# A planner's keys set anew in a fused banded-attention and feed-forward kernel

## The chip, the cores and the metric

The kernel runs on one core of one Trainium2 chip. The metric is device time in microseconds (us): the median of three executions. A separate execution was profiled, and all rows below come from it.

## The reference

The inputs are q, k and v of shape (8 batches, 8 heads, 576 positions, head size 64), and two weight matrices of 512x2048 and 2048x512, all float32. Attention sees a causal band of 64 positions; its output, 4608 tokens of 512 numbers, goes through a feed-forward layer with a piecewise gate.

```python
scores = scale * np.matmul(q, k.transpose(0, 1, 3, 2))
mask = (rel >= 0) & (rel < 64)
scores = np.where(mask, scores, -1000000000.0)
attn = np.exp(scores - np.max(scores, axis=-1, keepdims=True))
attn = attn / (np.sum(attn, axis=-1, keepdims=True) + 1e-09)
x = np.matmul(attn, v)            # to (4608, 512), heads side by side
h = x @ w_in
g = np.where(h >= 1, h, np.where(h <= -1, 0.0, (h + 1) ** 2 / 4))
out = g @ w_out
```

## The kernel before

**Work.** The tokens are 9 tiles of 512 (t = 0 to 8). Attention goes in 36 steps of 128 tokens (s = 0 to 35), four to a tile. The feed-forward layer has 16 slices of 128 hidden numbers (f = 0 to 15). Each float32 matrix is split into a high and a low part, and a product is three matmuls: high by high, high by low, low by high.

**Tiles 0 to 2** run plainly: for each f, `ffn_in` (12 matmuls, L1153, into the two buffers ps_h), then on ScalarE and VectorE relu, square, *gate* (L1175, VectorE; it reads ps_h and so gives it back), `ffn_high` (L1180, gh), `ffn_low` (L1185, gl), then `ffn_out` (12 matmuls, L1199). While tile 0 runs, the raw weights of each f are loaded and split on ScalarE and VectorE (`w_rest` L342, `w_sign` L319, two limits L323, shift L335, join L346, `w_high` L290, `w_low` L358). While tiles 1 and 2 run, 32 *half-sums* of weights (`add_sums`: `sum_whole` L842, `sum_sums` L849, `sum_high` L290 into o, `sum_low` L857, on VectorE or GpSimd) are made and stored to DRAM (`kept`): 16 *passes* `sum_pass` (L824, three transfers each) and two stores for each half-sum (L861, L862).

**Tiles 3 to 8** run in three blocks of two tiles with a scheme of seven products in place of eight (`ffn_product` L928, `out_product` L1014). Their right operands come from `kept` through a ring of seven slots (`ring_load`, L908). What they multiply is made out of four pairs of attention steps (r = 0 to 3) by `add_build` (`x_take`, `x_sums` L587, `x_high`, `x_low` L623); the first product of a block waits for all four.

**Attention steps** from s = 5 on: loads of q, k (L407, L411) and two of v (L417); scores on TensorE (L439); per head half a mask and minimum on VectorE (L462), exp on ScalarE (L482); inverse (L493, L494), normalise (L501), transposition (L508) on VectorE; a write to DRAM and a read back (L519, L522); then the values on TensorE (L552). In tile 2 and the blocks the values of one step stand on TensorE right behind the scores of a later one.

**Order.** Each engine and the queue of SyncE (SP) works in program order, and that order comes from a planner (`Plan.run`) that walks a model with fixed costs before anything is emitted. Each piece of work has a *key*. For each engine the planner takes, among pieces that could start at most PATIENCE after the earliest, the one with the lowest key:

```python
until = min(could)[0] + PATIENCE[e]
c = min((c for c in could if c[0] <= until), key=lambda c: c[1:])
```

Key 0 is the start of tile 0; `step(t)` is 21.33, 42.67 and 64 for t = 1, 2 and 3, that is 1.333 for each f, and block u begins at `64 + 2 * u * H_STEP`. The keys of attention steps are counted backwards from the tile that needs them: in tile 2 the last step (s = 11) has `step(2) - A_END - B_STEP - EARLY_2` and each one before it B_FIRST less; for the first block the last step has `64 - A_SUPER[0][0]`, each one before it `A_SUPER[0][1]` less. Loads of q and k have the step's key less L_LEAD, those of v V_LATE or V_LATE_2 more than that. Half-sum c of pass n (0 to 15) has `step(1) + S_LATE + S_PACE * (n + c / 2)`, the pass that of c = 0. A raw weight load has `W0_KEY + W0_STEP * (f + unit / 2)`.

The first k and the first raw weights are issued on ScalarE's queue ahead of all else; in the planner they are SP work that does nothing (`load_k(s) if s else None`, `FIRST_LOAD`).

Of the kernel before, what the change touches and what calls it, by code (L numbers as in the profile page):

```python
# [40 lines left out]
JOIN = 8  # L41
BEHIND = 2
E_SPAN = 0.29
E_LEAD = 9.81
W_LEAD = -1.5
W_FIRST = (17.22, -2.0, 1.41, 1.48, -3.05)
W_STEP = 1.02
L_LEAD = -0.77
W_LATE = (3.72, -1.06, -2.67, 7.19, 13.28, 13.03, 18.55)
W_LOAD = 1400  # L50
Q_LOAD = 700
K_LOAD = 1040
V_LATE = 2.92
W0_KEY = -100.2
FIRST_LOAD = 0, (0,)
M_LATE = 1
W0_STEP = 12.29
FINE = 4
NWARM = 8
A_FIRST = (-102.6, -95.58, -95.43, -95)  # L60
A_NEXT = 1.57
A_STEP = 4.75
A_SPAN = 2.18
A_LEAD = 4.64
O_LAG = 2.79
O_LAG_DMA = 2300
# [11 lines left out]
B_PE = 2210  # L78
B_DUE = (2.44, -1.28, -0.74)
B_STEP = 5.68  # L80
B_FIRST = 1.45
A_END = 5.86
V_PE = 1270
NORM = dict(Pool=800, DVE=480), dict(DVE=610)
G_LATE = (1.94, 1.65, -4.21, -4.45, 2.08)
D_LATE = (-0.7, 0.46, 6.3, -3.34, 6.37, 0.12)
# [11 lines left out]
SUM_KEEP = 1150  # L98
V_LATE_2 = 14.69
PATIENCE = dict(ACT=300, DVE=0, Pool=303, PE=0, SP=0)  # L100
# [5 lines left out]
SUPERS = 3  # L106
H_STEP = 18.67
S_LATE = 1.62
S_PACE = 2.47
O_CHANGE = 3.33, 3.2, 4.7  # L110
EARLY_2 = 2.71
A_SUPER = ((7.71, 2.68), (9.52, 4.03))
A_ORDER = (0, 4, 1, 5, 2, 6, 3, 7)
BUILD = (-12.04, 16.74)
X_SLOTS = 4, 0, 6, 1, 2, 3
# [3 lines left out]
WRITES = (1, None), (2, 1), (0, None), (3, 2), (3, 3), (1, 2), (2, 2)  # L119
R_LEAD = -4.99  # L120
R_LOAD = 430
L_DVE = 4, 6, 8
G_LEAD = (3.99, -2.67, 0.94, -2.12)
OP_LEAD = 10.45
D_LEAD = 0.72


class Plan:
# [10 lines left out]
    def add(self, key, cost, do, after=(), takes=(), gives=(), lag=0, shared=False):  # L139
        self.work.append((key, cost, do, set(after), takes, gives, lag, shared))  # L140
        return len(self.work) - 1
# [77 lines left out]
def banded_attention_then_ffn(ctx: ExitStack, tc: tile.TileContext, q, k, v, w, masks, out, out_t, dims):  # L219
# [142 lines left out]
    def add_weights(f, units):  # L362
        g = f, units
        m = len(units) * DM
        act, high, join, low, small = 105 + .916 * m, 92 + .844 * m, 10 + 1.22 * m, 67 + 1.05 * m, 90 + .25 * m
        key = f * W_STEP - (W_FIRST[f] if f < len(W_FIRST) else W_LEAD) + .5 * units[0]
        x = add(W0_KEY + W0_STEP * (f + .5 * units[0]), dict(SP=W_LOAD * len(units)), lambda e: None if g == FIRST_LOAD else w_load(g), lag=DMA_LAG)
        xr = add(key - W_LATE[0], dict(ACT=act), lambda e: w_rest(g), [x], takes=["u"])
        x = add(key, dict(ACT=act), lambda e: w_sign(g), [xr])
        x = add(key - W_LATE[1], dict(DVE=small), lambda e: w_limit_signed(g), [x])  # L370
        x = add(key - W_LATE[2], dict(DVE=small), lambda e: w_limit_unsigned(g), [x])
        x = add(key - W_LATE[3], dict(DVE=small), lambda e: w_shift(g), [x])
        x = add(key - W_LATE[4], dict(DVE=join), lambda e: w_join(g), [x])
        x = add(key - W_LATE[5], dict(ACT=high), lambda e: w_high(g, e), [x])
        x = add(key - W_LATE[6], dict(DVE=low), lambda e: w_low(g), [x], gives=[("u", xr)])
        for u in units:
            w_ready[f, u] = x
# [290 lines left out]
    def add_step(t, i):  # L668
# [7 lines left out]
        if s < FIRST:  # L676
            key = due = A_FIRST[s]
        elif s >= JOIN:
            key = a_keys[s]
        else:  # L680
            key = a_keys[s]
            due = min(key + A_SPAN, soon(s))
        lk = key - L_LEAD
        apart = A_SUPER[t > PLAIN][1]
        if s == 0:
            last["r"] = add(lk, dict(ACT=480), lambda e: round_masks())
        if s == PE_STEPS - 2:
            last["m"] = add(lk + M_LATE, dict(SP=590), lambda e: load_masks(), lag=DMA_LAG)
        late = s >= JOIN
        xq = add(lk, dict(SP=Q_LOAD), lambda e: load_q(s), takes=["qt"], lag=Q_LAG if late else DMA_LAG)  # L690
        xk = add(lk, dict(SP=Q_LOAD if late else K_LOAD), lambda e: load_k(s) if s else None, takes=["kt"], lag=K_LAG if late else DMA_LAG)
        vk, vl = lk + (V_LATE_2 if late else V_LATE), V_LAG if late else DMA_LAG
# [58 lines left out]
        else:  # L751
            dk = key if s >= JOIN else min(key + E_SPAN, soon(s) - E_LEAD)
            due = [dk + B_DUE[0], dk + B_DUE[0] + B_DUE[2]]
            x = [add(due[h], dict(DVE=LOWEST), lambda e, h=h: att_masked(s, h), [xs, last["m"]], gives=[(ps, xs, h)]) for h in range(2)]
            x = [add(due[h], dict(ACT=EXP[1]), lambda e, h=h: att_exp(s, h, False), [x[h]]) for h in range(2)]
            x = add(due[1], dict(DVE=430), lambda e: att_inverse(s, BOTH), x)
            x = [add(due[1], dict(DVE=870, Pool=1650) if s >= JOIN else dict(DVE=870), lambda e: att_normalize(s, BOTH, e), [x], shared=True)]
            due = dk + B_DUE[1]
            if s == SOON:
# [444 lines left out]
    def out_late(t, q, i):  # L1204
        if t < PLAIN - 1 or q < NF - 2:
            return O_LAG
        return O_CHANGE[0] if q == NF - 2 else O_CHANGE[1 + i // 2]
# [27 lines left out]
    def soon(s):  # L1235

        t, i = s * SB // TMAX, s * SB % TMAX // SB
        return step(t) + (FRONT * TMAX / 2 / 384 if 2 * i >= TMAX // SB else 0) - A_NEXT + i % 2

# [187 lines left out]
```

## Time and profile before

| | |
|---|---|
| median of three executions | 840.55 us (840.16 to 840.74) |
| the profiled execution's own time | 843.4 us |
| its span, first to last instruction | 841.6 us |
| TensorE busy | 821.6 us, 98% |
| VectorE busy | 687.0 us, 82% |
| ScalarE busy | 533.5 us, 63% |
| GpSimd busy | 213.8 us, 25% |
| moved by DMA | 216.08 MB, mean 257 GB/s |

In the rows PE is TensorE, PEld its weight loads, DVE VectorE, ACT ScalarE, POOL GpSimd, and SPq the queue of SyncE. Busy times come from one profiled execution, which took 2.85 us longer than the median. "Idle before" is the time an engine stood still before an instruction, with what ended it.

### The profile page before, as it was taken

The numbers are of one execution on the slowest core, as the hardware profiler recorded it, in microseconds if no ns is written. First come the engines' busy times: TensorE is split into PE (matmuls) and PEld (weight loads), VectorE is DVE, ScalarE is ACT, GpSimd is POOL, SyncE is SP. The second block draws the span as 40 slices with busy tenths as digits, with TensorE's granted clock in tenths as the row PEclk, the third lists the DMA queues.
The fourth block names the chain that finished last, engine by engine and source line by source line (L and its number), as shares of the span: only waits on it lengthen the run. The fifth ranks groups of instructions, "written<-read, shape, count | busy, mean of one in ns | idle before, by whom it ended". The sixth has DMA issues, their size and how long they took to land.

```text
span 841.6 us, 18582 instructions
## 1 busy us (share of the span) xinstructions
PE 821.6 (98%) x6588; PEld 672.1 (80%) x6588; DVE 687.0 (82%) x1613; ACT 533.5 (63%) x1303; POOL 213.8 (25%) x226
## 2 busy tenths in 40 slices
PE   7889999999999999999999999999999999999998
PEld 5767788878787878788888888888888888888886
DVE  6999996468757789888899986888999848878964
ACT  5999983545654764756775654777756536566442
POOL 1000014335664636221233320122332201100100
PEclk8999999999999999999999999999999999999999
DMA  8994359996788797788898898888888877777775
GB/s 322 394 375 170 100 165 331 362 331 200 214 265 262 219 285 235 271 252 272 272 333 253 284 316 281 269 268 282 302 252 244 294 230 198 192 195 193 198 224 164
DMA packets 151901, 216.08 MB, mean 257 GB/s; under 512 B 11904, under 2 KB 75264, under 8 KB 151808
## 3 DMA queue, kind: packets, MB, share of 16 engines
q1 hardware_dynamic: 151520, 213.97, 80.2%
q8 instruction: 53, 0.87, 0.4%
q10 hardware_dynamic: 288, 0.92, 0.3%
q14 instruction: 40, 0.33, 0.1%
HBM read 163.72 MB, written 51.12 MB: 255 GB/s over the span
## 4 chain that ended last, share of the span: by engine, by line
PE 75%; DVE 10%; DMA 7%; ACT 3%; issue 2%; POOL 2%; SPq 1%; ACTq 0%; POOLq 0%; DVEq 0%
PE acc L1014 27%; PE ps_h L928 14%; PE acc L928 14%; PE ps_h L1153 8%; PE acc L1199 7%; DMA kept<-u 4%; PE ps_a L439 2%; DVE u L842 1%; PE ps_a L552 1%; DVE u L857 1%; PE ps_h L552 1%; DVE u L849 1%; DMA raw<-in_w 1%; DVE wts L358 1%; DMA kt<-in_k 1%
## 5 line engine op out<-in xcount | busy, mean ns | idle before, releaser
L1014 PE MATMUL acc<-op,wts 128*128 128x512 f32 x576 | 137.7, 390 | 0.0
L1153 PE MATMUL ps_h<-xh,wts 128*128 128x512 f32 (+1 forms) x424 | 131.2, 376 | 6.1 <-DVE a L1175 4.4
L290 ACT CAST op<-g 128x512 fp32r<-128x512 f32 x129 | 80.2, 622 | 77.4 <-PE acc L1014 49.3
L1014 PEld LDWEIGHTS acc<-op,wts 128*128 128x128 f32 x576 | 107.8, 188 | 22.5
L1199 PE MATMUL acc<-wts,gh 128*128 128x512 f32 x384 | 120.1, 394 | 0.7 <-ACT gh L1180 0.7
L482 ACT ACTIVATE sm<-sm,nm 128x96 f32<-128x96 f32 x248 | 89.5, 363 | 12.3 <-DVE nm L462 11.6
L1153 PEld LDWEIGHTS ps_h<-xh,wts 128*128 128x128 f32 x424 | 78.0, 190 | 22.6 <-DVE a L1175 6.5
L1005 DVE TENSOR_TENSOR op<-g,op 128x512 fp32r<-128x512 f32 x107 | 76.7, 718 | 20.7 <-ACT op L290 20.2
L928 PE MATMUL ps_h<-wts 128*128 128x512 f32 x360 | 92.0, 391 | 0.0
L928 PE MATMUL acc<-wts 128*128 128x512 f32 x360 | 91.5, 389 | 0.0
L1199 PEld LDWEIGHTS acc<-wts,gh 128*128 128x128 f32 x384 | 70.8, 188 | 16.0 <-ACT gh L1180 1.1
L1168 ACT ACTIVATE a<-a 128x512 f32<-128x512 f32 (+1 forms) x125 | 77.1, 617 | 3.8
L1153 PE MATMUL ps_h<-xl,wts 128*128 128x512 f32 (+1 forms) x212 | 78.8, 372 | 0.6 <-DVE xl L565 0.6
L928 PEld LDWEIGHTS acc<-wts 128*128 128x128 f32 x360 | 67.5, 188 | 14.2
L928 PEld LDWEIGHTS ps_h<-wts 128*128 128x128 f32 x360 | 67.2, 188 | 14.2
L1199 PE MATMUL acc<-wts,gl 128*128 128x512 f32 x192 | 75.3, 392 | 1.4 <-DVE gl L1185 1.4
L1163 ACT ACTIVATE a<-g 128x512 f32<-128x512 f32 x96 | 60.5, 630 | 19.4 <-DVE g L943 14.0
L1175 DVE SCALAR_TENSOR_TENSOR g<-a,g 128x512 f32<-128x512 f32 x96 | 68.1, 716 | 3.8 <-ACT a L1168 3.2
L1005 POOL TENSOR_TENSOR op<-g,op 128x512 fp32r<-128x512 f32 x28 | 36.1, 1295 | 129.5 <-ACT op L290 118.1
L1185 POOL TENSOR_TENSOR gl<-a,gh 128x512 fp32r<-128x512 f32 (+1 forms) x34 | 48.6, 1429 | 45.0 <-ACT gh L1180 43.2
L992 DVE TENSOR_TENSOR g<-g 128x512 f32<-128x512 f32 x83 | 58.4, 717 | 0.5
L1175 DVE SCALAR_TENSOR_TENSOR a<-a,ps_h 128x512 f32<-128x512 f32 (+1 forms) x53 | 33.3, 628 | 25.1 <-ACT a L1168 24.9
(145 smaller groups left out, 1544.5 us busy)
## 6 DMA issues: line engine op xcount, KB each, us to landing
wts<-kept SPq DMA_DIRECT2D x240, 256.0 KB, 3.6
vt<-in_v SPq DMA_DIRECT2D x72, 256.0 KB, 4.9
ptd<-moved SPq DMA_DIRECT2D x31, 512.0 KB, 4.7
kt<-in_k SPq DMA_DIRECT2D x35, 384.0 KB, 5.1
kept<-wts SPq DMA_DIRECT2D x48, 256.0 KB, 4.8
gh<-kept SPq DMA_DIRECT2D x48, 256.0 KB, 3.7
gl<-kept SPq DMA_DIRECT2D x48, 256.0 KB, 3.6
raw<-in_w SPq DMA_DIRECT2D x12, 1023.8 KB, 10.6
```

Of the source, the lines that this page charges most:

```text
L290: nc.scalar.copy(dst, src)
L482: nc.scalar.activation(t, t, AF.Exp, bias=nm[:, g:g + 1], scale=-1.0, accum_out=den[:, g:g + 1])
L928: nc.tensor.matmul(ps, lhsT=r[:, part, cp], rhs=x_op(k, xp)[:, cp], start=j in (0, 1, 3, 4) and i == 0 and cp == 0, stop=j in (1, 2, 5, 6) ...
L992: engine[eng].tensor_tensor(out=g[:, out], in0=g[:, a], in1=g[:, b], op=op)
L1005: engine[eng].tensor_tensor(out=low, in0=g_of(n)[:, of], in1=high.bitcast(F32), op=ALU.subtract)
L1014: nc.tensor.matmul(opened[b][m], lhsT=r[:, part, m], rhs=op[xp], start=j in (0, 1, 3, 4) and i == 0 and n == 0, stop=j in (1, 2, 5, 6) and ...
L1153: nc.tensor.matmul(ps, lhsT=wts[f, 0][:, part, c * P:(c + 1) * P], rhs=x[:, c, r], start=(c == 0 and j == 0), stop=(c == NP - 1 and j == 2),)
L1163: nc.scalar.activation(gs[t, f, r.start][0], phs[t, f, r.start], AF.Relu, bias=0.5, scale=0.5)
L1168: nc.scalar.activation(a, a, AF.Square)
L1175: nc.vector.scalar_tensor_tensor(out=ps if t >= PLAIN else a, in0=a, scalar=1.0, in1=ps, op0=ALU.min, op1=ALU.max)
L1185: engine[eng].tensor_tensor(out=g[2], in0=g[0], in1=g[1].bitcast(F32), op=ALU.subtract)
L1199: nc.tensor.matmul(acc[t, i][:, n], lhsT=g[:, sub], rhs=wts[f, 1][:, part, n], start=(q == 0 and j == 0), stop=(q == NF - 1 and j == 2 and ...
```

## The change

No instruction is added or removed and no buffer changes: the constants from which the keys come are set anew, and some are split in two. `AHEAD` gives the first q, the first k and the first raw weights the three lowest keys of SP in the model. Steps below 8 and steps from 8 on get constants of their own (L_LEAD_1 and L_LEAD, B_DUE_1 and B_DUE), tile 0 its own O_LAG_1; A_SHIFT is eight zeros. The diff, whole:

```diff
--- before.py
+++ after.py
@@ -42,27 +42,31 @@
 BEHIND = 2
 E_SPAN = 0.29
 E_LEAD = 9.81
-W_LEAD = -1.5
-W_FIRST = (17.22, -2.0, 1.41, 1.48, -3.05)
-W_STEP = 1.02
-L_LEAD = -0.77
-W_LATE = (3.72, -1.06, -2.67, 7.19, 13.28, 13.03, 18.55)
+W_LEAD = -1.6
+W_FIRST = (17.22, -2.0, 1.41, 1.48, -3.05, -1.6, -1.6, -1.6, -1.6, -1.6, -1.6, -1.6, -1.6, -1.6)
+W_STEP = 1.01
+L_LEAD = -0.32
+L_LEAD_1 = -0.85
+W_LATE = (3.72, -0.68, -2.67, 7.19, 13.28, 13.54, 18.55)
 W_LOAD = 1400
 Q_LOAD = 700
 K_LOAD = 1040
 V_LATE = 2.92
-W0_KEY = -100.2
+W0_KEY = -100.41
 FIRST_LOAD = 0, (0,)
 M_LATE = 1
-W0_STEP = 12.29
+AHEAD = -10000
+W0_STEP = 12.53
 FINE = 4
 NWARM = 8
 A_FIRST = (-102.6, -95.58, -95.43, -95)
-A_NEXT = 1.57
-A_STEP = 4.75
-A_SPAN = 2.18
-A_LEAD = 4.64
-O_LAG = 2.79
+A_SHIFT = (0, 0, 0, 0, 0, 0, 0, 0)
+A_NEXT = 1.68
+A_STEP = 4.76
+A_SPAN = 2.99
+A_LEAD = 5.22
+O_LAG = 2.84
+O_LAG_1 = 2.79
 O_LAG_DMA = 2300
 DMA_LAG = 1300
 BEGIN = dict(PE=1500, ACT=2300, DVE=2500, SP=2400)
@@ -76,13 +80,14 @@
 EXP = 1545, 1440
 S_PE = 1230, 1150
 B_PE = 2210
-B_DUE = (2.44, -1.28, -0.74)
-B_STEP = 5.68
-B_FIRST = 1.45
-A_END = 5.86
+B_DUE = (3.56, -1.32, -6.48)
+B_DUE_1 = (2.44, -0.88, 1.53)
+B_STEP = 5.96
+B_FIRST = 1.42
+A_END = 5.87
 V_PE = 1270
 NORM = dict(Pool=800, DVE=480), dict(DVE=610)
-G_LATE = (1.94, 1.65, -4.21, -4.45, 2.08)
+G_LATE = (1.89, 1.65, -0.34, -4.45, 2.17)
 D_LATE = (-0.7, 0.46, 6.3, -3.34, 6.37, 0.12)
 TURN = 965, 1500
 HOP_SP = 690, 460
@@ -96,7 +101,7 @@
 STORE_LAG = 3500
 SUM_PASS = 1950
 SUM_KEEP = 1150
-V_LATE_2 = 14.69
+V_LATE_2 = 11.54
 PATIENCE = dict(ACT=300, DVE=0, Pool=303, PE=0, SP=0)
 BUFS = dict(qt=2, kt=2, vt=4, ps_a=2, sm=2, ptd=3, pt2=1, x=2, u=2, ps_h=2, a=2, gh=2, gl=2, acc=4, o=2, tmp=2)
 BUFS.update({n: 1 for n in ("xtmp", "xs0", "xs1", "xs2", "xs3", "xs4", "xs5", "X", "Y")}, raw=4, ring=7, op=5)
@@ -104,25 +109,25 @@
 
 PLAIN = 3
 SUPERS = 3
-H_STEP = 18.67
-S_LATE = 1.62
-S_PACE = 2.47
+H_STEP = 18.71
+S_LATE = 5.52
+S_PACE = 2.31
 O_CHANGE = 3.33, 3.2, 4.7
-EARLY_2 = 2.71
-A_SUPER = ((7.71, 2.68), (9.52, 4.03))
+EARLY_2 = 5.98
+A_SUPER = ((7.61, 2.95), (9.49, 4.39))
 A_ORDER = (0, 4, 1, 5, 2, 6, 3, 7)
-BUILD = (-12.04, 16.74)
+BUILD = (-10.06, 20.9)
 X_SLOTS = 4, 0, 6, 1, 2, 3
 G_FIRST = 8
 RING_SLOT = 7
 PARTS = (0, 0, 0), (1, 1, 1), (0, 5, 4), (1, 3, 2), (0, 4, 3), (1, 6, 5), (0, 2, 6)
 WRITES = (1, None), (2, 1), (0, None), (3, 2), (3, 3), (1, 2), (2, 2)
-R_LEAD = -4.99
+R_LEAD = -14.28
 R_LOAD = 430
 L_DVE = 4, 6, 8
-G_LEAD = (3.99, -2.67, 0.94, -2.12)
-OP_LEAD = 10.45
-D_LEAD = 0.72
+G_LEAD = (4.7, -3.24, 0.04, -2.49)
+OP_LEAD = 12.59
+D_LEAD = 1.3
 
 
 class Plan:
@@ -364,7 +369,7 @@
         m = len(units) * DM
         act, high, join, low, small = 105 + .916 * m, 92 + .844 * m, 10 + 1.22 * m, 67 + 1.05 * m, 90 + .25 * m
         key = f * W_STEP - (W_FIRST[f] if f < len(W_FIRST) else W_LEAD) + .5 * units[0]
-        x = add(W0_KEY + W0_STEP * (f + .5 * units[0]), dict(SP=W_LOAD * len(units)), lambda e: None if g == FIRST_LOAD else w_load(g), lag=DMA_LAG)
+        x = add(W0_KEY + W0_STEP * (f + .5 * units[0]) if g != FIRST_LOAD else AHEAD + 2, dict(SP=W_LOAD * len(units)), lambda e: None if g == FIRST_LOAD else w_load(g), lag=DMA_LAG)
         xr = add(key - W_LATE[0], dict(ACT=act), lambda e: w_rest(g), [x], takes=["u"])
         x = add(key, dict(ACT=act), lambda e: w_sign(g), [xr])
         x = add(key - W_LATE[1], dict(DVE=small), lambda e: w_limit_signed(g), [x])
@@ -674,21 +679,25 @@
         pt, pv = ("ps_h", "acc") if s < LENT else ("ps_a", "ps_a")
         ps = "acc" if s < FIRST and s % 2 else "ps_a"
         if s < FIRST:
-            key = due = A_FIRST[s]
+            key = A_FIRST[s]
+            due = key + A_SHIFT[s]
         elif s >= JOIN:
             key = a_keys[s]
         else:
             key = a_keys[s]
-            due = min(key + A_SPAN, soon(s))
-        lk = key - L_LEAD
+            due = min(key + A_SPAN, soon(s)) + A_SHIFT[s]
+        lk = key - (L_LEAD if s >= JOIN else L_LEAD_1)
         apart = A_SUPER[t > PLAIN][1]
         if s == 0:
             last["r"] = add(lk, dict(ACT=480), lambda e: round_masks())
         if s == PE_STEPS - 2:
             last["m"] = add(lk + M_LATE, dict(SP=590), lambda e: load_masks(), lag=DMA_LAG)
         late = s >= JOIN
+        if s == 0:
+            lk = AHEAD
         xq = add(lk, dict(SP=Q_LOAD), lambda e: load_q(s), takes=["qt"], lag=Q_LAG if late else DMA_LAG)
-        xk = add(lk, dict(SP=Q_LOAD if late else K_LOAD), lambda e: load_k(s) if s else None, takes=["kt"], lag=K_LAG if late else DMA_LAG)
+        xk = add(lk + (s == 0), dict(SP=Q_LOAD if late else K_LOAD), lambda e: load_k(s) if s else None, takes=["kt"], lag=K_LAG if late else DMA_LAG)
+        lk = key - (L_LEAD if s >= JOIN else L_LEAD_1)
         vk, vl = lk + (V_LATE_2 if late else V_LATE), V_LAG if late else DMA_LAG
         xv = add(vk, dict(SP=Q_LOAD), lambda e: load_v(s, 0), last["v"], takes=["vt"], lag=vl)
         xw = add(vk, dict(SP=Q_LOAD), lambda e: load_v(s, 1), [xv], takes=["vt"], lag=vl)
@@ -749,13 +758,14 @@
                 ready.append(x)
             gives = [("ptd", taken[0]), ("ptd", taken[1])]
         else:
-            dk = key if s >= JOIN else min(key + E_SPAN, soon(s) - E_LEAD)
-            due = [dk + B_DUE[0], dk + B_DUE[0] + B_DUE[2]]
+            dk = key if s >= JOIN else min(key + E_SPAN, soon(s) - E_LEAD) + A_SHIFT[s]
+            late_by = B_DUE if s >= JOIN else B_DUE_1
+            due = [dk + late_by[0], dk + late_by[0] + late_by[2]]
             x = [add(due[h], dict(DVE=LOWEST), lambda e, h=h: att_masked(s, h), [xs, last["m"]], gives=[(ps, xs, h)]) for h in range(2)]
             x = [add(due[h], dict(ACT=EXP[1]), lambda e, h=h: att_exp(s, h, False), [x[h]]) for h in range(2)]
             x = add(due[1], dict(DVE=430), lambda e: att_inverse(s, BOTH), x)
             x = [add(due[1], dict(DVE=870, Pool=1650) if s >= JOIN else dict(DVE=870), lambda e: att_normalize(s, BOTH, e), [x], shared=True)]
-            due = dk + B_DUE[1]
+            due = dk + late_by[1]
             if s == SOON:
                 z = add(due - 2, dict(Pool=600), lambda e: att_clear(), early_values)
                 last["d"] = [add(due - 2, dict(SP=HOP_SP[0]), lambda e, j=j: att_zero(j), [z], lag=HOP_LAG[0]) for j in range(2)]
@@ -1203,7 +1213,7 @@
 
     def out_late(t, q, i):
         if t < PLAIN - 1 or q < NF - 2:
-            return O_LAG
+            return O_LAG if t else O_LAG_1
         return O_CHANGE[0] if q == NF - 2 else O_CHANGE[1 + i // 2]
 
     os = {}
```

## Rows read from the trace of the kernel before

**Rows 1.** Busy time of each engine in stretches of the span. After each engine its busy us and (x instructions), then the granted clock of TensorE, the DMA share and GB/s. The first two are the start, the next three the rest in order up to the last matmuls, the last two the parts of 128:346.

```profile
0.00:20.00 20.00, 14.21 (x161) 11.46 (x162) 12.60 (x34) 11.50 (x42) 2.91 (x16) 0.83 0.89 318
20.00:40.00 20.00, 16.90 (x205) 14.87 (x204) 17.68 (x47) 18.49 (x58) 0.00 (x0) 0.91 1.01 394
...
40.00:128.00 88.00, 84.74 (x725) 67.26 (x725) 86.72 (x200) 80.40 (x173) 5.92 (x5) 1.00 0.59 210
128.00:346.00 218.00, 213.71 (x2059) 174.10 (x2062) 158.85 (x466) 125.53 (x356) 110.00 (x125) 1.00 0.86 266
346.00:837.40 491.40, 491.40 (x3460) 404.25 (x3450) 409.81 (x867) 297.61 (x679) 94.94 (x82) 1.00 0.82 254
...
128.00:180.00 52.00, 52.00 (x366) 43.67 (x365) 28.57 (x73) 26.36 (x61) 16.41 (x19) 1.00 1.09 352
180.00:346.00 166.00, 161.71 (x1695) 130.43 (x1698) 130.28 (x393) 99.18 (x295) 93.59 (x106) 1.00 0.79 238
```

**Rows 2.** What TensorE waited for: the first three rows are of 35 to 70 us, the last three of 180 to 347 us. Us in total, times, longest.

```profile
PE acc L1199 <- DVE gl L1185: 1.4, 3, 0.9
PE ps_h L1153 <- DVE a L1175: 1.1, 2, 1.0
PE acc L1199 <- ACT gh L1180: 0.7, 1, 0.7
...
PE ps_h L1153 <- DVE a L1175: 3.3, 4, 1.6
PE ps_a L439 <- PE acc L1199: 0.7, 1, 0.7
PE ps_a L439 <- DVE nm L462: 0.3, 1, 0.3
```

**Rows 3.** The issues of the SP queue in the first microseconds: start us, us, what.

```profile
0.74 0.39 SPq L407 DMA_DIRECT2D qt<-in_q  x1
1.19 0.42 SPq L417 DMA_DIRECT2D vt<-in_v  x1
...
3.58 0.43 SPq L309 DMA_DIRECT2D raw<-in_w  x1
7.26 0.33 SPq L407 DMA_DIRECT2D qt<-in_q  x1
```

**Rows 4.** TensorE in order of time, at the places the text names: start us, us, what, [idle before].

```profile
128.35 0.39 PE L1153 MATMUL ps_h<-xh,wts 128*128 128x512 f32 x1
...
153.33 1.00 PE L439 MATMUL ps_a<-kt,qt 64*32 64x96 f32 x64
...
187.32 0.50 PE L1153 MATMUL ps_h<-xh,wts 128*128 128x512 f32 x1 [0.86 <-DVE a L1175]
...
312.86 0.50 PE L1153 MATMUL ps_h<-xh,wts 128*128 128x512 f32 x1 [1.63 <-DVE a L1175]
...
346.41 1.66 PE L928 MATMUL ps_h<-wts 128*128 128x512 f32 x6
```

**Rows 5.** VectorE in order of time, at the places the text names.

```profile
39.60 0.62 DVE L323 TENSOR_SCALAR raw<-raw 128x512 int16<-128x512 int16 x2
...
126.60 1.56 DVE L358 TENSOR_TENSOR wts<-u,wts 128x1024 fp32r<-128x1024 f32 x1
...
185.41 0.69 DVE L857 TENSOR_TENSOR u<-u,o 128x512 fp32r<-128x512 f32 x1 [0.73 <-ACT o L290]
...
310.91 0.42 DVE L842 TENSOR_TENSOR u<-wts 128x256 f32<-128x256 f32 x1 [2.59 <-DMA kept<-u]
...
337.57 0.69 DVE L857 TENSOR_TENSOR u<-u,o 128x512 fp32r<-128x512 f32 x1 [0.69 <-ACT o L290]
...
340.09 1.46 DVE L587 TENSOR_TENSOR u<-raw 128x256 f32<-128x256 f32 x2 [1.23 <-ACT raw L290]
```

**Rows 6.** The SP queue from 122 to 150 us, the rows of passes (L824) up to the next load of v (L417).

```profile
122.77 6.88 SPq L824 DMA_DIRECT2D kept<-wts  x9
...
133.60 1.83 SPq L824 DMA_DIRECT2D kept<-wts  x3
...
138.27 7.00 SPq L824 DMA_DIRECT2D kept<-wts  x9
...
146.56 2.55 SPq L824 DMA_DIRECT2D kept<-wts  x3
149.15 0.59 SPq L417 DMA_DIRECT2D vt<-in_v  x1
```

**Rows 7.** The SP queue's own waits over the whole span, two of them, and from the DMA issues the ring loads' row (KB each, median us to landing).

```profile
SPq L908 <- PE acc L1014: 102.6, 125, 1.8
...
SPq L407 <- PE ps_a L439: 25.8, 11, 5.2
...
wts<-kept SPq DMA_DIRECT2D x240, 256.0 KB, 3.6
```

**Rows 8.** One line's instructions on both engines: x count, ns least/median/most, first and last start in us.

```profile
L849 DVE TENSOR_TENSOR u<-u x74: 273/291/1423, 130.4 to 336.6; 128x128 f32<-128x128 f32 x74
L849 POOL TENSOR_TENSOR u<-u x54: 452/462/1322, 127.2 to 325.1; 128x128 f32<-128x128 f32 x54
```

**Rows 9.** A stretch of the chain of work that ended last: start us, us, what.

```profile
761.88 75.50 PE acc L1014 x333
```

## The prediction

> **What bounds the kernel now.** I read the busy times by stretch first, because a share over the whole span mixes stages. From 346 us to the last matmul TensorE is busy 491.40 us of 491.40 [rows 1], and a matmul of 512 columns takes 75.50 us / 333 = 0.2267 us there [rows 9]. No order of the same work makes that stretch shorter; it can only get longer. What another order can win lies ahead of it: TensorE stands idle 88 - 84.74 = 3.26 us from 40 to 128 us and 218 - 213.71 = 4.29 us from 128 to 346 us, 7.55 us together, and 40 - 31.11 = 8.89 us in the first 40 us [rows 1].
>
> Then I read what each idle time waited for. From 180 us on it is mostly the gate: four times, 3.3 us, with 0.7 + 0.3 us at the first block's door [rows 2]. The two largest are 0.86 us at 187.32 and 1.63 us at 312.86 [rows 4]. In VectorE's own order the reader sees the same cause each time: a piece of a half-sum stands in the queue ahead of the gate and waits itself, 0.73 us for ScalarE's o at 185.41 and 2.59 us for a store of `kept` at 310.91 [rows 5]. From 35 to 70 us the 3.2 us are waits for gh, gl and the gate [rows 2], in a stretch where VectorE is busy 86.72 us of 88 [rows 1]: there TensorE waits because VectorE is full, not because something is badly placed.
>
> TensorE's busy share overstates how full it is. Where it never waits, weight loads are busy 404.25 / 491.40 = 82.3% of the time; in 128:346 it is 79.9%, in 40:128 76.4% [rows 1]. The Trainium skill (Perfetto Trace Analysis, Identifying the Most-Contended Engine) says that matmul busy time is no good measure of the distance to the roofline and that the busy share of weight loads is one. By that rule the two stretches lose 218 - 174.10 / 0.823 = 6.5 us and 88 - 67.26 / 0.823 = 6.3 us, 12.8 us to be won in place of 7.55. I keep the idle times for the sum, since other matmul shapes in these stretches move that share too.
>
> **The map.** Slice f = 15 of tile 0 (key 20) starts at 128.35 us and block 0 (key 64) at 346.41 [rows 4]: 218.06 / 44 = 4.96 us for each unit of key. It holds in between: scores of step 9, key 25.52, should fall at 155.7 us and start at 153.33 [rows 4].
>
> **The change, part by part.** Every instruction stays; only its place can move, so each part costs what it uncovers.
>
> *First three transfers, zeros, copies.* The old keys of SP are q at -101.83, k with it (the tie goes to q, added first), raw weights at -100.2, then v at -98.91. With AHEAD the same three come first, and the queue shows what follows: q, v, ... raw at 3.58 [rows 3]. Next in key, q of step 3 goes from -94.23 to -94.15 and the second raw load from -94.055 to -94.145: still in that order. A_SHIFT is zero; W_FIRST repeats W_LEAD. Cost 0. What bounds it: a swap of those two would matter little, as the third q waits for its buffer until 7.26 us anyway [rows 3]. The 8.89 us of the start stay.
>
> *Tile 0 (G_LATE, W_LATE, W0_STEP, O_LAG_1, A_LEAD, A_SPAN, B_DUE_1).* The gate's key goes from 1.333 f - 4.21 to 1.333 f - 0.34, so that up to two limit steps of weights (0.62 us for two [rows 5]) come ahead of it; weights get done that much sooner. VectorE's work up to 128 us is the same, and the last `w_low` runs 126.60 to 128.16 with f = 15 starting at 128.35 [rows 4, 5]. What TensorE saves early it would wait for there, unless VectorE's idle time shrinks, and that is 88 - 86.72 = 1.28 us. Bounds: -1.28 us, and +2.5 us if each of the four waits for gate or gl grows by 0.62. I take 0, nearest to the row of a full VectorE.
>
> *Tile 2's steps, v, half-sums.* These move together. Step 9 goes from key 25.52 to 22.02 (17 us earlier), steps 8 to 11 all by 3.5 units. V of step 9 goes from 25.52 + 0.77 + 14.69 = 40.98 to 22.02 + 0.32 + 11.54 = 33.88. Passes went from 22.95 in steps of 2.47, so eight lay ahead of that v, 24 transfers; the queue shows 9 + 3 + 9 + 3 = 24 before it at 149.15 [rows 6]. Now they begin at 26.85 in steps of 2.31, and four lie ahead. The first half-sum moves 3.90 units (19 us) later, the last from 61.24 to 62.66 (7 us later). So attention of tile 2 comes into 128:180, where VectorE works 28.57 us of 52, and leaves 180:346, where it works 130.28 of 166; early half-sums go the other way. The gates that waited at 187.32 and 312.86 stood behind half-sums that met a full queue of passes and stores or a busy ScalarE. I take both waits as gone, 0.86 + 1.63 = 2.49 us, and one new wait of about the mean of the two smaller ones, (3.3 - 2.49) / 2 = 0.4. Term: -2.1 us. Bounds: -4.29 (all idle time of the stretch) and +2.5 (three more waits of the mean, 3.3 / 4 = 0.82).
>
> *The first block's door (BUILD, A_SUPER, S_PACE).* Step 12 goes from 37.53 to 35.74, step 19 stays (56.29, 56.39). The build of r = 0 goes from 51.96 to 53.94, those of r = 1 to 3 to 74.8, 95.7 and 116.6; like before these stand behind all half-sums. Cost 0 while the last half-sum ends before the last pair of values is there; now `sum_low` starts at 337.57, and the build's first subtraction waits for ScalarE until 340.09 [rows 5]. If that cover is gone, see the second rival.
>
> *Blocks (R_LEAD, H_STEP, G_LEAD, OP_LEAD, D_LEAD, B_DUE).* Nothing to win. Ring loads lose 9.29 units against loads of q, k and v. They wait for a slot, not for the queue (102.6 us behind L1014, none over 1.8 [rows 7]). Seven slots are 7 x 6 x 0.2267 = 9.5 us of work, a load lands in 3.6, and the longest wait of a q load at the queue's head is 5.2 [rows 7]: 0.7 us to spare. Cost 0; without that spare, 5.2 for each second wait in a row.
>
> **The sum.** 0 + 0 - 2.1 + 0 + 0 = -2.1 us: the profiled execution's 843.4 would be 841.3. It lies 2.85 us over the median; against the median the same step gives 840.55 - 2.1 = 838.4.
>
> **Rivals.** *One: idle time only changes place.* Half-sums, gates and stores are the same in number, each half-sum keeps its chance to stand before a gate. For it: the waits are small and scattered, four in 166 us. Against: the cause of the largest is a queue that this change clears. 840.5 us.
>
> *Two, slower: half-sums reach the first block's door.* Between the build's start and the first product lie 346.41 - 340.09 = 6.3 us [rows 4, 5]. If the last `sum_low` moves with its key by 7 us, to about 344.6 and done by 345.3, the build follows it and the product starts near 351.6, 5.2 us late: 840.55 - 2.1 + 5.2 = 843.7, or 845.8 without the gain. It decides from about 340 us on. Against it: a half-sum starts when its buffers are free, whatever its key, if VectorE has nothing else.
>
> *Three, slower: VectorE and GpSimd collide more.* The 128-column step of a half-sum takes 273 ns at best and 1423 at worst on VectorE [rows 8], and GpSimd works 32% of 128:180 but 56% of 180:346 [rows 1]. Half-sums pushed into the second stretch meet it more often: three more gate waits of 0.82 us are +2.5, 843.0. The Trainium skill (SBUF — State Buffer, Who interferes with whom) has the rule: an instruction of VectorE with two SBUF inputs and one of GpSimd that reads SBUF lock each other out for a whole instruction.
>
> *Four, slower: a ring load stands behind a q load.* Two such waits in a row are about 845.
>
> **How the numbers follow.** Forecast 0.50 (its own range 835.0 to 838.8); rival one 0.29; two 0.13; three 0.05; four 0.03. A measurement of this kernel tells 0.2% (1.7 us) from no change. So faster 0.50, same 0.29, slower 0.21. The range goes down to 834.5, which is 6 us of the 7.55, and up to 844.3, which holds rival two with the gain; about 1 in 10 is left out on either side.
>
> **What would show it.** Right: V of step 9 after some 12 transfers of passes, scores of step 9 near 138 to 143 us, idle time of TensorE in 128:346 near 2.2 us, and a first product near 344 us. The start up to 35 us as it was. Wrong: a first product after 348 us with half-sums after 340 (rival two); any wait of TensorE after 346 us (rival four); f = 15 of tile 0 much earlier or later than 128.35, which would mean that tile 0's order weighed more than I give it.

## The result, and the profile after

| | before, same chip | after |
|---|---|---|
| median of four executions | 840.64 us (840.16 to 841.16) | 844.58 us (843.94 to 846.99) |
| the profiled execution | | 843.94 us, span 841.9 us |
| TensorE, VectorE busy | | 820.0 us (97%), 692.7 us (82%) |
| ScalarE, GpSimd busy | | 529.5 us (63%), 204.7 us (24%) |

The ratio is 1.0055 (95% interval 1.0041 to 1.007): slower, by 3.9 us between the medians and 4.6 by the ratio, where I had forecast 2.1 us less. The time lies outside the range too, which went up to 844.3.

The profile that the forecast was made from has to be put right first. It took 843.4 us, 2.85 over its median. I therefore had the kernel before profiled a second time (r1 below, 840.63 us, span 837.8). Where before is compared with after below, it is this second execution that is meant, and its rows are shown. Busy time by stretch, columns as in [rows 1], first the second execution of before:

```profile
20.00:40.00 20.00, 15.20 (x200) 12.89 (x197) 19.28 (x51) 18.94 (x60) 0.00 (x0) 1.00 1.02 413
40.00:128.00 88.00, 85.71 (x728) 68.11 (x728) 85.96 (x198) 79.53 (x170) 6.39 (x5) 1.00 0.61 214
128.00:180.00 52.00, 52.00 (x378) 43.38 (x384) 28.47 (x74) 25.75 (x60) 16.46 (x19) 1.00 1.09 356
180.00:346.00 166.00, 163.85 (x1723) 132.55 (x1714) 132.98 (x412) 103.11 (x313) 93.32 (x106) 1.00 0.80 242
```

and the kernel after:

```profile
20.00:40.00 20.00, 16.31 (x210) 13.85 (x209) 19.26 (x50) 18.72 (x60) 0.00 (x0) 1.00 1.01 394
40.00:128.00 88.00, 85.72 (x670) 68.28 (x668) 86.03 (x191) 76.61 (x154) 2.92 (x4) 1.00 0.59 210
128.00:180.00 52.00, 49.82 (x474) 41.42 (x472) 27.44 (x85) 27.90 (x75) 18.17 (x20) 1.00 1.09 352
180.00:346.00 166.00, 162.84 (x1661) 132.18 (x1662) 136.28 (x423) 104.43 (x319) 81.00 (x87) 1.00 0.81 248
346.00:837.40 491.40, 490.06 (x3419) 402.88 (x3418) 409.51 (x854) 289.02 (x650) 99.74 (x82) 1.00 0.80 251
```

Read the first number after each length. TensorE's idle time from 128 to 346 us is 2.15 us in the second execution of before, not the 4.29 of [rows 1]: half of what I counted on from this stretch was one execution's chance. After, it is 2.18 + 3.16 = 5.34 us, and 1.34 us more come behind 346, where [rows 1] had none. 6.68 - 2.15 = 4.5 us; the spans differ by 4.1, the medians by 3.9. From 40 to 128 us the two kernels stand idle equally long (2.28 us after, 2.29 before); in the start they still run in the same order (below), and after 100 us the granted clock of both is 1.00. So the whole loss comes after 128 us, and it lies in five waits.

**The five waits.** What TensorE waited for from 100 to 850 us (us, times, longest), before and then after:

```profile
PE ps_h L1153 <- DVE a L1175: 1.5, 2, 0.9
PE ps_a L439 <- DVE nm L462: 0.3, 1, 0.3
PE ps_a L439 <- PE acc L1199: 0.3, 1, 0.3
```

```profile
PE ps_h L1163 <- DVE a L1185: 2.3, 2, 1.2
PE ps_h L557 <- DMA ptd<-moved: 1.7, 1, 1.7
PE acc L1209 <- POOL gl L1195: 1.4, 1, 1.4
PE ps_h L938 <- DMA gh<-kept: 1.3, 1, 1.3
```

(Lines of after stand 5 to 10 further down: the gate L1175 is L1185.) Gone are waits for the gate that ended at 185.52 and 309.44 us (0.65 and 0.87), the ones that [rows 4] show at 187.32 and 312.86, and both at the door. New are these. They belong to the order and not to one execution: r2 below, which has after's order on every engine but SP, shows the first four again, with 1.4, 1.3, 1.3 and 1.3 us, and the fifth with 0.4.

*At 155 us: the gate, behind a half-sum on ScalarE.* ScalarE and VectorE in order of time:

```profile
152.75 1.28 ACT L295 CAST o<-u 128x512 fp32r<-128x512 f32 x2 [3.88 <-DMA out<-o]
153.94 0.59 ACT L1173 ACTIVATE a<-ps_h 128x512 f32<-128x512 f32 x1
...
155.29 0.69 DVE L1185 SCALAR_TENSOR_TENSOR a<-a,ps_h 128x512 f32<-128x512 f32 x1 [0.54 <-ACT a L1178]
```

The half-sum's cast needs an `o`; both are taken by output stores. ScalarE stands 3.88 us at it, until the first of the two lands, and relu, square and gate of the next slice queue behind. TensorE loses 1.2 us.

*At 179 us: the values of step 9, behind passes.* From the chain that ended last, and the pass from SP's queue:

```profile
165.66 0.89 DVE sm L513
...
168.99 0.98 SPq L524
170.02 4.87 DMA moved<-sm
174.96 5.58 DMA ptd<-moved
180.68 1.15 PE ps_h L557 x32
```

```profile
163.32 3.84 SPq L834 DMA_DIRECT2D kept<-wts  x6
```

The probabilities are ready by 166.55, but the write is not issued before 168.99, behind two passes and the two stores of a half-sum; write and read then take 4.87 and 5.58 us beside the passes' transfers. 1.7 us lost.

*At 252 us: the gate, behind ScalarE's `o` again.* 1.1 us:

```profile
250.55 0.58 ACT L295 COPY o<-acc 128x512 f32<-128x512 f32 x1 [1.54 <-DVE u L859]
...
252.40 0.69 DVE L1185 SCALAR_TENSOR_TENSOR a<-a,ps_h 128x512 f32<-128x512 f32 x1 [1.02 <-ACT a L1178]
```

```profile
245.26 0.46 SPq L1237 DMA_DIRECT2D out<-o  x1
```

The row names a piece of a half-sum on VectorE, which happens to end at 250.40. What the copy needs is an `o`: the output store issued at 245.26 takes 5.23 us to land, until 250.49, and the copy starts at 250.55. In r2 the same store lands at 251.32 and the copy starts at 251.39, and with a third `o` (r5 below) the wait is 0.2 us. So this is the mechanism of 155 us a second time.

*At 341 us: gl on GpSimd, beside VectorE's build.*

```profile
333.43 1.29 POOL L1195 TENSOR_TENSOR gl<-a,gh 128x512 fp32r<-128x512 f32 x1 [0.53 <-ACT gh L1190]
339.68 2.88 POOL L1195 TENSOR_TENSOR gl<-a,gh 128x512 fp32r<-128x512 f32 x1 [1.26 <-ACT gh L1190]
```

```profile
340.01 0.74 DVE L628 TENSOR_TENSOR wts<-u,wts 128x256 fp32r<-128x256 f32 x2
```

The same operation takes 1.29 us at 333 and 2.88 at 340, where VectorE is already in a chain of operations with two inputs (339.41 to 341.44). TensorE loses 1.4 us. Such a neighbour alone does not make GpSimd slow:

```profile
259.55 1.29 POOL L1195 TENSOR_TENSOR gl<-a,gh 128x512 fp32r<-128x512 f32 x1 [5.47 <-ACT gh L1190]
259.59 2.05 DVE L506 TENSOR_TENSOR sm<-sm,den 128x768 f32<-128x768 f32 x1
```

Here GpSimd began first, and VectorE's operation is the long one (it takes 1.06 us at 164.00). That the chain of VectorE is what held GpSimd up at 340 is read from these rows; no run takes it apart.

*At 363 us: a ring load.* SP's queue, then the chain:

```profile
358.34 0.53 SPq L527 DMA_DIRECT2D ptd<-moved  x1
358.93 0.46 SPq L918 DMA_DIRECT2D gh<-kept  x1
```

```profile
358.93 6.07 DMA gh<-kept
365.13 0.93 PE ps_h L938 x3
```

It is issued behind a read-back of 512 KB and takes 6.07 us to land, where the median of the 240 in [rows 7] is 3.6. 1.3 us lost. That read-back is not shown to be the cause: the transfers issued from 355.81 to 364.41 us all take 5.0 to 6.6 us, in a stretch (350 to 365 us) with a DMA share of 0.95.

The five have four mechanisms. That raises the question for the experiments: did the moves do this, each by its own merit, or does any new order do it?

### The profile page after: what moved, and what is told of

The parts are those of the page before. It is cut to its first block, busy times and chain, and to the rows that moved or that the text cites. A ratio compares the mean times of both kernels' runs of the same rounds, so it can differ in the third digit from the quotient of the medians.

```text
span 841.9 us, 18577 instructions
## 1 busy us (share of the span) xinstructions
PE 820.0 (97%) x6588; PEld 670.6 (80%) x6588; DVE 692.7 (82%) x1636; ACT 529.5 (63%) x1297; POOL 204.7 (24%) x209
## 4 chain that ended last, share of the span: by engine, by line
PE 75%; DVE 9%; DMA 7%; ACT 5%; issue 2%; POOL 1%; SPq 0%; ACTq 0%; POOLq 0%; DVEq 0%
PE acc L1024 27%; PE ps_h L938 13%; PE acc L938 13%; PE ps_h L1163 7%; PE acc L1209 7%; DMA kept<-u 3%; PE ps_a L444 3%; DMA out<-o 2%; ACT sm L487 1%; PE ps_a L557 1%; PE ps_h L557 1%; PE acc L557 1%; DVE u L852 1%; DVE sm L506 1%; DVE wts L363 1%
## 5 line engine op out<-in xcount | busy, mean ns | idle before, releaser
L295 ACT CAST op<-g 128x512 fp32r<-128x512 f32 x122 | 76.0, 623 | 82.3 <-PE acc L1024 49.8
L1185 DVE SCALAR_TENSOR_TENSOR g<-a,g 128x512 f32<-128x512 f32 x96 | 67.1, 705 | 3.0 <-ACT a L1178 2.6
L1015 POOL TENSOR_TENSOR op<-g,op 128x512 fp32r<-128x512 f32 x26 | 33.6, 1294 | 111.6 <-ACT op L295 102.4
L1002 POOL TENSOR_TENSOR g<-g 128x512 f32<-128x512 f32 x15 | 19.8, 1318 | 141.3 <-DVE op L1015 63.7
```

The source lines that it names most:

```text
L295: nc.scalar.copy(dst, src)
L1002: engine[eng].tensor_tensor(out=g[:, out], in0=g[:, a], in1=g[:, b], op=op)
L1015: engine[eng].tensor_tensor(out=low, in0=g_of(n)[:, of], in1=high.bitcast(F32), op=ALU.subtract)
L1185: nc.vector.scalar_tensor_tensor(out=ps if t >= PLAIN else a, in0=a, scalar=1.0, in1=ps, op0=ALU.min, op1=ALU.max)
```

## The experiments

**What differs at all.** In the traces the instructions of the two kernels come in the same order, engine by engine, up to 88 us on VectorE, 92 on ScalarE, 101 on TensorE, 109 on SP and 114 on GpSimd. (By the planner the two halves of one attention step's mask and exp change places before that; in the rows they look alike.) With all other constants put back, AHEAD and A_SHIFT leave the order of before on every engine.

**Before again (r1), and the ring's key put back (r2).**

> The kernel before, unchanged, for a second trace of it. Theory A (the profiled execution behind rows 1 to 9 was itself slow at its start, by chance): its own time is near 840.6, and slice f = 15 of tile 0 starts 1.5 to 3 us earlier than 128.35, since the emitted order of before and after is the same on every engine up to about 100 us and after's trace is 1.7 us earlier there. Theory B (after really is earlier in tile 0): f = 15 starts near 128.3 again. Timed against itself: 840.6, within 0.1%.

> The kernel after with R_LEAD alone put back to -4.99. The emitted order differs from after's on the SP queue only. Theory A (the wait of 1.3 us for a ring load at 364 us in after's trace is a loss that nothing gives back): 1.3 us less than after, 843.2, and no wait of TensorE after 346 us. Theory B (the loss of 3.9 us lies ahead of the blocks, and the ring wait is taken up by a later one or was chance): 844.5, as after.

```diff
-R_LEAD = -14.28
+R_LEAD = -4.99
```

r1: 1.0001 (0.999 to 1.0012), by theory A. r2: 1.0050 (1.0032 to 1.0068). In r2 the ring's wait shrinks from 1.3 to 0.4 us and TensorE's idle time after 100 us goes from 6.68 to 5.73, but the gain in time is inside the interval. The ring's key is at most a small part.

**Groups of constants alone (r3, r4, r8).** Each is the kernel before with one group of after's values: the blocks' (`H_STEP, A_SUPER, BUILD, R_LEAD, G_LEAD, OP_LEAD, D_LEAD, B_DUE`); tile 0's (`W_*, W0_*, L_LEAD_1, A_NEXT, A_STEP, A_SPAN, A_LEAD, G_LATE, B_DUE_1`); tile 2's (`S_LATE, S_PACE, EARLY_2, B_STEP, B_FIRST, A_END, V_LATE_2, O_LAG, L_LEAD`).

> The kernel before with the block constants alone as after has them (H_STEP, A_SUPER, BUILD, R_LEAD, G_LEAD, OP_LEAD, D_LEAD and B_DUE). Theory A (ring wait and the wait at the first block's door, 1.3 + 1.4 us in after's trace, belong to this group): 843.3. Theory B (the loss belongs to tile 2's steps and the half-sums): 840.6, as before.

> The kernel before with the constants of tile 0 and of steps 4 to 7 alone as after has them (the W constants, L_LEAD_1, A_NEXT, A_STEP, A_SPAN, A_LEAD, G_LATE, B_DUE_1). Up to about 100 us its order is before's. Theory A (this group is not what costs): 840.6, within 0.1%. Theory B (the kernel before is a picked order, and any new order costs about as much, whichever constants made it): 843 to 845.

> The kernel before with the constants of tile 2's steps and of the half-sums alone as after has them (S_LATE, S_PACE, EARLY_2, B_STEP, B_FIRST, A_END, V_LATE_2, O_LAG, L_LEAD). Theory A (a merely different order costs): 1.002 to 1.008. Theory B (this group makes after's waits at 154.6 and 178.8 us, 1.4 and 1.9 us): 1.004, with TensorE idle 3 to 4 us between 128 and 180 us. My prediction's step, that this group wins: 0.9975.

| | ratio (95%) | on 840 us | TensorE idle after 100 us |
|---|---|---|---|
| r3, blocks | 1.0106 (1.009 to 1.0122) | +8.9 | 7.99 |
| r4, tile 0 | 1.0041 (1.0028 to 1.0055) | +3.4 | 3.10 |
| r8, tile 2 | 1.0176 (1.0156 to 1.0195) | +14.8 | 10.70 |
| after, all | 1.0055 (1.0041 to 1.007) | +4.6 | 6.68 |

(r4's profiled execution took 840.41 us, against a median of 843.73.) r3 and r8 came out slower than either of their theories said, r4 as its theory B. The groups alone sum to +27.1, together they give +4.6: their costs don't add. So no group can be given a share of the loss. What TensorE waited for most in r3 and, in two rows, in r8:

```profile
PE ps_h L1163 <- DVE a L1185: 5.3, 4, 2.3
```

```profile
PE acc L938 <- DMA gh<-kept: 5.1, 1, 5.1
PE acc L1209 <- ACT gh L1190: 4.6, 1, 4.6
```

**One key, by next to nothing (r7, r12).** The kernel before with

```diff
-W_STEP = 1.02
+W_STEP = 1.01
```

> The kernel before with W_STEP 1.01 in place of 1.02 and nothing else: no key of the weights moves by more than 0.15 units, and yet the emitted order differs from before's from about 105 us to the end. Theory A (the order of before is a picked one, and an order that is merely different costs some us wherever it comes from): 1.002 to 1.006. Theory B (what costs is where these constants put tile 2's steps, the half-sums and the ring loads): within 0.1% of before.

and, apart from it, with

```diff
-EARLY_2 = 2.71
+EARLY_2 = 2.8
```

> The kernel before with EARLY_2 2.80 in place of 2.71 and nothing else (tile 2's steps 0.09 units, 0.4 us, earlier in the keys): the emitted order differs from before's from about 150 us on. Theory A (before is a picked order and a merely different one costs): slower by 2 to 12 us, 1.002 to 1.014. Theory B (only large moves of keys cost): within 0.1% of before.

r7: 1.0149 (1.013 to 1.0168), 12.5 us. r12: 1.0117 (1.0103 to 1.0131), 9.8 us. Neither key has a merit of that size; r12 is within its theory A, r7 slower than it. Both drew the same new wait, which r8 has too, the first row r7's, the second r12's:

```profile
PE acc L928 <- DMA gh<-kept: 5.1, 1, 5.1
```

```profile
PE acc L928 <- DMA gh<-kept: 5.2, 1, 5.2
```

r7's chain that ended last, and SP's queue:

```profile
349.99 1.36 PE ps_h L928 x6
351.35 1.37 PE acc L1199 x6
352.79 0.60 ACT o L290
...
354.35 4.30 DMA gh<-kept
358.78 2.90 PE acc L928 x6
```

```profile
352.68 1.06 SPq L1227 DMA_DIRECT2D out<-o  x2
353.84 0.40 SPq L522 DMA_DIRECT2D ptd<-moved  x1
354.35 0.45 SPq L908 DMA_DIRECT2D gh<-kept  x1
```

The last six matmuls of tile 2's `ffn_out` stand behind the block's first products. The load into that ring slot is issued only after their output store and a read-back, and lands 4.30 us later. r12 and r8 show the same chain (loads of 4.36 and 4.29 us).

The wait costs more than its 5.1 us. The row of r7 from the end of the wait, columns as in [rows 1]:

```profile
358.78:364.09 5.31, 5.31 (x13) 4.14 (x14) 1.44 (x3) 1.85 (x3) 0.00 (x0) 0.50 1.02 383
```

TensorE had stood still, and its granted clock is 0.50 there, the lower level of 1.2 GHz: six matmuls take 2.90 us in place of 1.36. Half of 5.31 us is 2.7 us more, so that this place costs 7.8 of r7's 12.5 us; worked out alike it is 8.1 of 9.8 in r12.

**The door opened (r9, r15).** r9 is r7 with those six matmuls further ahead:

```diff
-O_CHANGE = 3.33, 3.2, 4.7
+O_CHANGE = 3.33, 2.0, 2.0
```

> The kernel with W_STEP 1.01 alone (12.5 us slower than before), with O_CHANGE set so that the last piece of tile 2's last ffn_out stands ahead of three products in place of behind them: TensorE's order differs in that one place, SP's behind it. In the trace of the first of the two the sixth product waits 5.1 us for a ring load into gh, which can only be issued once that last piece has read gh, and SP issues it behind the store of that tile. Theory A (that one place costs it): no wait for gh<-kept at 353 us and 4 to 5 us less, 1.0095 of before. Theory B (the wait moves to the next thing that the door needs): under 1.5 us less, 1.013 to 1.015.

1.0100 (1.0085 to 1.0114) in place of 1.0149: 4.1 us back, as theory A had it. The wait does not go, it falls from 5.1 to 3.0, and behind it the granted clock stays at 1.00, which gives back the 2.7 us too. (In exchange r9's trace has 1.7 us of half clock behind another wait, at 156 us.) So the place of these matmuls does set the wait, and it accounts for at least part of r7's loss.

**A third `o` (r5 on after, r6 on before).** With `name="o", bufs=3`, room being found by moving two small constants; the order stays.

> The kernel after with three buffers o in place of two (the planner still counts two, so that the emitted order of every engine is after's; the room comes from two small early tiles that now lie in the slot of the last weights). In after's trace ScalarE waits for a store out<-o at 148 to 153 us and at 249 us, the gate stands behind it, and TensorE loses 1.4 and 1.3 us at 154.6 and 251.8. Theory A (the wait for o is the cause): both waits are gone and the time falls by 2 to 2.7 us, to 1.0025 of before. Theory B (the next thing in ScalarE's or VectorE's queue waits in its place): the ratio stays near 1.0055.

> The kernel before with the same three buffers o and before's order: the control for the run with after's order. Theory A (a wait for o costs only where after's order puts it ahead of a gate): within 0.1% of before. Theory B (a third o helps any order by as much): 2 us less than before, 0.9975.

r5: 1.0057 (1.0036 to 1.0078), by theory B. r6: 0.9996 (0.9983 to 1.0009), by theory A. In r5 the wait at 252 nearly goes (1.1 to 0.2 us) and so does the one at 179 (1.7 to 0.3), but the one at 155 grows from 1.2 to 2.0, and the ring's from 1.3 to 2.6:

```profile
PE ps_h L938 <- DMA gh<-kept: 2.6, 1, 2.6
```

Idle time after 100 us is 6.51 in place of 6.68. At 155 the third `o` moves the wait only to the next half-sum, which stands behind the same stores:

```profile
154.71 0.62 ACT L295 CAST o<-u 128x512 fp32r<-128x512 f32 x1 [4.87 <-DMA out<-o]
```

Taking one wait's cause away let others grow by as much.

**No passes (r10 on after, r11 on before).** `sum_pass` issues nothing; the ring reads another part of the same size for what the passes would have brought.

> The kernel after without the 48 transfers of the passes (the ring loads that would read them read a half-sum's part in their place, so this part of the result is left out); all other orders are after's. Theory A (the waits at 154.6 us, for a store of o, and at 178.8 us, for the read-back, are long because the passes fill the queue and the DMA engines, 1.09 busy there): both gone, TensorE idle under 0.5 us from 128 to 180 us, 2 to 3.3 us less than after: 1.0015 to 1.003 of before. Theory B (they come from the order alone): idle 1.5 us or more there, within 0.1% of after's 1.0055.

> The kernel before without the same 48 transfers (the same part of the result left out): the control. TensorE has no idle time from 128 to 180 us in before, so Theory A: 0 to 1 us less than before, 0.999 to 1.0. Theory B (the passes cost every order as much): 2 us or more less, 0.9976.

r10: 1.0038 (1.0024 to 1.0053). r11: 0.9983 (0.9973 to 0.9994). Without passes TensorE is busy 52.00 us of 52.00 from 128 to 180 in after: both waits there, 155 and 179, go. But before gains as well, since both its gate waits go too (0.37 us of idle time left), and the two still stand 0.55% apart. What is left in r10 are the later waits:

```profile
PE ps_h L938 <- DMA gh<-kept: 1.3, 1, 1.3
PE ps_h L1163 <- DVE a L1185: 1.2, 1, 1.2
PE acc L1209 <- POOL gl L1195: 1.1, 1, 1.1
```

So the passes' transfers cause the two waits of 128:180 in after and the two gate waits of before. They do not cause the other three, and without them the kernels differ by as much as the intervals can tell (idle time by 3.3 us in place of 4.5).

**Passes spread (r13 on after, r14 on before), and with the door (r15).** The pass is issued right behind the first store of its half-sum instead of where the planner puts it:

```diff
-xp = add(key, dict(SP=SUM_PASS), lambda e: sum_pass(l, n), ready, ...)
+xp = add(key, dict(SP=SUM_PASS), lambda e: None, ready, ...)
...
-x = add(k, ..., lambda e, c=c: sum_keep(l, n, c), [x], ...)
+x = add(k, ..., lambda e, c=c: (sum_keep(l, n, c), sum_pass(l, n) if c == 0 else None), [x], ...)
```

> The kernel after with each pass issued behind the first stores of its own half-sum in place of as soon as the weights are there: the same 48 transfers, spread from 130 to 340 us; only SP's order changes. Theory A (the passes in one lump delay the store of o and the read-back): no wait of TensorE at 154 and 179 us, 1.5 to 3 us less than after, 1.0025 to 1.0035 of before. Theory B (the transfers cost as much later, ahead of ring loads and read-backs there): within 0.1% of after's 1.0055.

> The kernel before with the passes spread in the same way. Without the passes before took 0.9983 of its time. Theory A (it is their lump that costs): 0.998 to 0.9995, and no wait for a gate at 184 and 308 us. Theory B (before's order was fitted with the lump in it, and any move costs): 1.001 or more.

> The kernel after with the passes spread and, beside that, the last ffn_out of tile 2 ahead of one more product (O_CHANGE 2.0; TensorE's order differs from after's in that place alone). Theory A (the door's place costs as in the kernel with the small key step): the ring wait at 363 us is gone and the time is 1 to 1.5 us under that of the kernel with the passes spread alone. Theory B (here the piece waits for gl on GpSimd, and the product had filled that wait): the same or up to 1.5 us more, with a longer wait for gl at 341 us.

r13: 1.0119 (1.0104 to 1.0135). r14: 1.0044 (1.0031 to 1.0056). r15: 1.0122 (1.0106 to 1.0137). Worse in each. The waits at 155 and 179 us are gone, as theory A of r13 had it, but others come, most of them from 247 to 347 us; r14 is as its theory B, r15 as fast as r13 with other waits than either theory named. The largest in r13 and in r15:

```profile
PE ps_a L557 <- DMA ptd<-moved: 3.1, 1, 3.1
```

```profile
PE ps_a L557 <- DVE den L498: 2.8, 1, 2.8
```

**All runs together.** TensorE's idle time after 100 us in the profiled execution, and what half clock cost there: half of the time that TensorE worked at a granted clock of 0.50, an estimate from the clock in each trace.

| | idle, us | half clock, us | ratio |
|---|---|---|---|
| r11 | 0.37 | 0 | 0.9983 |
| r6 | 0.98 | 0 | 0.9996 |
| r1 | 2.15 | 0 | 1.0001 |
| r4 | 3.10 | 0 | 1.0041 |
| r10 | 3.68 | 0 | 1.0038 |
| r14 | 3.90 | 1.6 | 1.0044 |
| r2 | 5.73 | 0 | 1.0050 |
| r5 | 6.51 | 1.7 | 1.0057 |
| after | 6.68 | 0 | 1.0055 |
| r3 | 7.99 | 1.7 | 1.0106 |
| r15 | 8.60 | 3.4 | 1.0122 |
| r12 | 9.15 | 2.9 | 1.0117 |
| r9 | 9.31 | 1.7 | 1.0100 |
| r8 | 10.70 | 5.0 | 1.0176 |
| r13 | 11.37 | 1.7 | 1.0119 |
| r7 | 12.21 | 2.7 | 1.0149 |

Idle time alone misses: r8 has 8.6 us more of it than r1 and loses 14.8. The two columns together, less r1's 2.15, give the loss of each run within 1.7 us, but for r4, whose profiled execution took 3.3 us less than its median. Each fall of the clock came with a wait or just behind one or two (1.0 to 5.2 us long), but not every wait brought one: 2.4 us at 154 us in r7 and 3.0 at 359 in r9 did not.

And each of the ten other orders I ran of this same work (r2 to r4, r7 to r9, r12 to r15), like after itself, is slower than before's, whatever was moved. They are not eleven independent draws: r2, r13 and r15 are after's order with little moved, r14 is before's, r9 is r7's, and r7, r8 and r12 share one wait at the door. The two that are as fast or faster, r6 and r11, keep before's order and add a buffer or leave transfers out.

## Why the prediction was wrong, point by point

**What bounds the kernel.** Right in kind: after's loss is TensorE's idle time after 100 us (in slower orders the half clock behind long waits comes on top, which no term had). Wrong in size: the 4.29 us of [rows 1] was that one execution's. f = 15 of tile 0 starts at 128.35 us there and at 126.72 in the second; the granted clock in 20:40 was 0.91 there and 1.00 in the second. I took that execution's 2.85 us off the total at the end, but reckoned the term from its idle time, of which 2.1 us were part of the same excess. The 12.8 us by weight loads were not there either: their share from 128 to 346 us is 80.7% in the second execution and 79.9% in the first, with half the idle time.

**First three transfers: 0.** Right. They leave the order as it was.

**Tile 0: 0.** Right here: idle time from 40 to 128 us is the same within 0.01 us. But alone, these keys cost 3.4 us (r4), with nearly the whole stretch in unchanged order: a key of tile 0 shifts what the planner does later. That path was in no term. (The upper bound counted four waits for gate or gl; [rows 2] has five.)

**Tile 2's steps, v, half-sums: -2.1.** This step failed, and with it the forecast. Its first half held: both waits behind half-sums are gone. They were worth 0.65 + 0.87 us in the second execution, not 2.49. Its second half, "one new wait of about the mean of the two smaller ones", failed: new waits came at 155, 179 and 252 (1.2 + 1.7 + 1.1 us). The term measured 4.0 - 1.5 = +2.4 us in place of -2.1; the door, 1.4 - 0.6, and the blocks, 1.3, make up the rest of the 4.5. I had treated old waits as faults to be removed and new ones as leftovers. I had in fact moved attention into the stretch where passes fill DMA (its share 1.09 in 128:180, before and after), and had not asked which transfer would then be late there: the output stores that hold `o`, and the write and read-back of a step.

The working also took the key as the place. V of step 9 has 15 transfers of passes ahead of it at 137.34 us and 18 at 143.64, against 12 foretold; scores of step 9 are at 152.76, where I said 138 to 143 and before has 151.75. Step 8's scores went from 108.01 to 128.23, behind `ffn_in` of f = 15, and step 9 stands right ahead of step 8's values, which need step 8's read-back. A key is a wish; the last thing needed sets the place.

**The first block's door: 0.** The build was in time: first product at 342.95 against 342.58 before. But VectorE's build now ran ahead of and beside the last gl on GpSimd, 1.4 us. By these rows that is rival three's collision, at a place I had not looked: "what hides this work" was answered for the build's own end, not for its neighbour.

**Blocks: 0.** Failed by 1.3 us, in the place I had called short of cover, "0.7 us to spare": a load lands in 6.07 in place of 3.6, which eats that spare three times over. I had taken the median of the whole span for a stretch in which transfers take 5.0 to 6.6. The mechanism is near rival four's, with a read-back ahead in the queue in place of a q load. Its own price of about 845 was for two such waits in a row, and there was one.

**The rivals and chances.** "Idle time only changes place" had 0.29 and a change of zero. Its mechanism was the nearest: waits drawn anew. What it lacked is its sign. In an order with only 2 us of idle time little can go and much can come: a new draw of waits lies above the old one, not around it. Eleven orders, after among them, all slower by 0.4 to 1.8%, agree with that here. As these runs have it, that rival belonged 3 to 15 us on the slow side and not at 840.5.

**What stays open.** Whether an order exists that beats before's by more than the measurement can tell: r6, with before's order and a third `o`, has 0.98 us of idle time and a ratio inside its interval of 1, and none of the new orders came near. Why before's order is the better one: that its constants had been picked by measurement is an assumption of theory A in r4, r7 and r12, which no run shows. Why the groups' costs cancel as they do (27.1 alone, 4.6 together) is not traced wait by wait, and for r13 to r15 the waits are read, not separated.

## What to carry to other kernels

Where the bounding engine idles for 2 us of 840, a new order made by moved keys is to be read as a fresh draw of waits, and here every draw was worse; a forecast from each move's own merit had no hold on it. Before counting idle time as headroom, profile a second execution: here half of what one showed after 128 us was chance. Read the granted clock behind a long wait of TensorE too, since the wait can cost half as much again. And when a wait is removed, name for each stretch that receives the moved work the transfer, the buffer and the neighbouring engine that will be short there, and price that first.

## What the runs showed of the hardware that I had not expected

- The start differs between executions of the same program: a granted clock of 0.91 in 20:40 in one execution of before [rows 1], 1.00 in the other, and f = 15 1.6 us earlier in the second. The clock is not all of it: r11, in the same order up to there and with 0.91 in 20:40 as well, has f = 15 at 126.85 us, near the second's 126.72.
- GpSimd's `ffn_low` of 128x512 takes 1.29 us with VectorE idle (170.34 us) and also beside a two-input operation of VectorE that began after it, which then took 2.05 us in place of 1.06; it took 2.88 where it began in the midst of a chain of such operations. The Trainium skill (SBUF — State Buffer, Who interferes with whom) has the two engines lock each other out there; the trace agrees.
- A transfer of 256 KB that lands in 3.6 us in the median took 6.07 behind a read-back of 512 KB, among others that took 5.0 to 6.6.
- Behind the 5 us waits of r7, r8 and r12 TensorE's granted clock was 0.50 (1.2 GHz), and six matmuls took 2.90 us in place of 1.36.
